# Sharing the opening's normalisations with ScalarE in a fused linear-attention and SwiGLU kernel, with the second tiles turned sooner and the first products issued part by part

## The chip, the cores and the metric

The kernel runs on one core of a Trainium2 chip. The metric is device microseconds (us) of one execution, as the median of several. One profiled execution gives the trace that is read here.

## The reference

One sequence of 2048 tokens with 1024 features is normalised, then goes through two branches whose outputs are multiplied and added to the input. The change touches only the first rows of the work: the normalisation `xn` and the first products of the gate and up projections.

```python
x  = A_x                                   # [1, 2048, 1024], f32
xn = (x - mean(x)) / sqrt(var(x) + 1e-5)   # layernorm over the 1024 features, no weights
# branch B, SwiGLU with F = 3584
h  = silu(xn @ w1) * (xn @ w3)
g  = silu(h @ w2)
# branch A, linear attention with 32 heads of 32
q, k, v = split(xn @ wqkv)
phi(t)  = concat(softmax(t @ w_phi), softmax(-(t @ w_phi)))     # per head
o = phi(q) (phi(k)^T v) / (phi(q) sum(phi(k)) + 1e-6)
return x + (o @ wo) * g
```

## The kernel before

**Products.** Every large matrix is cut into two by two blocks, and a block product is made from seven smaller ones instead of eight (a Strassen-Winograd scheme). The seven left operands of the tokens are called A11, A12, S2, S1, S3, S4 and A22, the right operands of the weights B11, B21, T2, T1, T3, B22 and T4; `ORDER` lists them with the PSUM bank (`a`, `b` or `c`) in which each is summed. To come near f32 accuracy each operand is kept as a high part (a cast to the matrix engine's f32 form) and a low part (what the cast left out, by a subtraction), and a product is three passes: high by high, low of the weights by high of the tokens, and high of the weights by low of the tokens. With four slices of the contraction that makes 12 matmuls of 128x512 for each product. `gate_up(step)` issues the 12 matmuls of product number `step`, and the function that it returns (kept in `reads`) issues the instructions that read the bank afterwards. "Product n" below is `gate_up(n)`. Each slice `f` of 128 columns takes seven products, one for each of A11 to A22. Bank `a` has one buffer, `b` and `c` have two each.

**The opening.** Tokens come in tiles of 128 rows. Tiles 0 to 3 (`xs[0]` to `xs[3]`) give A11 (their first 512 features, half 0) and A12 (half 1); tiles 4 to 7 give A21 and A22, from which S1, S2, S3 and S4 are summed. For each tile VectorE takes the mean and variance (`stats`), then ScalarE a square root and VectorE five small instructions give the reciprocal deviation (`rstd`, one for each group of four tiles), then `norm` subtracts the mean and scales, one instruction for each half. TensorE turns each half (`turn`: four 128x128 transposes into a PSUM bank), ScalarE casts the high part (`early_turn`), VectorE subtracts for the low part (`early_low`), and ScalarE also keeps an f32 copy (`early_raw`, or `raw_x` for tiles 4 to 7), which frees the bank. 36 transposes into `banka` that nobody reads run before that. The weights' operands are split the same way: `first_cast` casts on ScalarE, `first_low` subtracts on VectorE or on GpSimd; `b_operand` does both. `gpsimd_behind(src)` makes GpSimd wait until `src` is normalised.

**Order.** Throughout the gate and up products each engine runs its instructions in the order in which the program writes them, and so the place of a line sets what stands behind what: an instruction that waits holds back all that follow it on its engine. `OPENING` fixes which product is which. Products 0 to 4 multiply A11 or A12 by the first weight slices, product 7 is the first with S1, product 10 the first with S2, 12 and 13 the two with S3.

Of the kernel before, what the change touches and what calls it, by code (L numbers as in the profile page):

```python
# [10 lines left out]
AF = mybir.ActivationFunctionType  # L11
# [16 lines left out]
def tile_kernel(ctx: ExitStack, tc: tile.TileContext, x, wkT, wqT, wv, wphi, wo, w1, w3, w2, out):  # L28
    nc = tc.nc
# [184 lines left out]
    def norm(mv, sd, j, xt, halves=range(2)):  # L214

        for a in halves:
            nc.vector.tensor_scalar(xt[a], xt[a], mv[:, j, 0:1], sd[:, 1, j:j + 1], op0=OP.subtract, op1=OP.mult)
# [419 lines left out]
    def gate_up(step):  # L637
# [18 lines left out]
        if first:  # L656
# [3 lines left out]
                    kept_banks[f] = turned[0] % 3  # L660
            else:
                bank[b] = ps.tile([P, 512], F, name=f"bank{b}", bufs=BANKS[b])
        n = 0
        for k in range(4):
            for u, w in PASSES:
                nc.tensor.matmul(bank[b], bos[tb, f][bn][:, w, k], ao[an][:, u, k], start=first and n == 0,  # L666
                                 stop=LAST[b] == an and n == 11, skip_group_check=True)
# [77 lines left out]
    def first_b(f, n):  # L745
        b_operand(bos[0, f], ("B11", "B21")[n], raw_b[f][:, n])

    def first_cast(f, n):
        t = bos[0, f][("B11", "B21")[n]] = quad("bo")
        nc.scalar.copy(t[:, 0], raw_b[f][:, n].rearrange("p (k n) -> p k n", n=P))  # L750
# [20 lines left out]
    def early_raw(t, h):  # L771
        raw[t][early_at(t, h)[0]] = raw_x(pts.pop((t, h)))
# [3 lines left out]
    warm = ps.tile([P, 512], F, name="banka", bufs=BANKS["a"])  # L776
    for k in range(36):
        nc.tensor.transpose(warm[:, :P], xs[2 + min(k // 8, 1)][k // 4 % 2][:, k % 4 * P:k % 4 * P + P], ident)
# [12 lines left out]
    first_low(1, 0, nc.gpsimd)  # L791
    first_low(0, 1, nc.gpsimd)
    for t in range(4):
        early_low(t, 0)
    reads = [gate_up(0)]
    for t in range(4):
        early_raw(t, 0)
    for t in range(4):
        norm(mvs[0], sd, t, xs[t], (1,))
    gpsimd_behind(xs[3][1])  # L800
    first_low(1, 1, nc.gpsimd)
    stats(mvs[1], 0, xs[4])
    for t in range(4):
        early_turn(t, 1, **(in_c if t == 0 else {}))
# [25 lines left out]
    for t in range(4):  # L830
# [334 lines left out]
    bos = {}  # L1165
# [552 lines left out]
```

## Time and profile before

| | us |
|---|---|
| median of 3 runs | 2339.92 (2339.9 to 2340.1) |
| profiled execution, its own time | 2342.56 |
| span of its instructions | 2339.0 |
| busy TensorE | 2320.3 (99% of the span) |
| busy VectorE | 1825.2 (78%) |
| busy ScalarE | 889.0 (38%) |
| busy GpSimd | 258.6 (11%) |

In rows of the timeline the first number is the start in us from the span's first instruction, the second the length, then the engine, the line of the program, the operation, what it writes and reads, how many alike follow each other, and in brackets the idle time before it with what ended it. PE is TensorE, DVE VectorE, ACT ScalarE, POOL GpSimd.

### The profile page before, as it was taken

The page shows a single profiled execution, that of the slowest core. Times are in us where ns is not written, and L with a number is a line of the kernel's source. Part 1 is how long each engine was busy: PE and PEld are TensorE (multiplying, and loading weights), DVE is VectorE, ACT ScalarE, POOL GpSimd, SP SyncE. Part 2 cuts the span into 40 slices and gives each one's busy share as a digit, 9 for nine tenths or more (in the row PEclk, how much of TensorE's full clock was granted, in tenths as well). Part 3 has the DMA queues.
Part 4 walks back from the last instruction along what each step waited for, and adds up shares of the span by engine and source line. Part 5 has one row for each costly group of instructions (what it writes and reads, how often), then busy time and mean ns, then how long its engine had stood idle before and what let it go on. Part 6 is the DMA issues. An engine that isn't in the chain of part 4 may idle for free.

```text
span 2339.0 us, 33900 instructions
## 1 busy us (share of the span) xinstructions
PE 2320.3 (99%) x12754; PEld 1901.1 (81%) x12754; DVE 1825.2 (78%) x2854; ACT 889.0 (38%) x1561; POOL 258.6 (11%) x208
## 2 busy tenths in 40 slices
PE   8999999999999999999999999999999999999999
PEld 6778877788888888888888788888888888887787
DVE  8877788885688888875577777778688888887784
ACT  6445444443345554543222122334443333353000
POOL 1000000000000000000000000332022222211652
PEclk9999999999999999999999999999999999999999
DMA  3456789997788888866988978996644654379863
GB/s 129 158 197 218 246 302 370 346 322 225 240 278 307 299 305 298 285 230 217 379 293 280 336 230 319 331 363 233 205 153 135 207 180 135 133 250 278 234 186 104
DMA packets 302883, 580.93 MB, mean 248 GB/s; under 512 B 24696, under 2 KB 157184, under 8 KB 300032
## 3 DMA queue, kind: packets, MB, share of 16 engines
q1 hardware_dynamic: 296384, 555.70, 70.6%
q10 hardware_dynamic: 6336, 23.07, 2.5%
q8 instruction: 100, 1.64, 0.3%
q14 instruction: 63, 0.52, 0.1%
HBM read 375.78 MB, written 202.91 MB: 247 GB/s over the span
## 4 chain that ended last, share of the span: by engine, by line
PE 93%; DMA 3%; DVE 2%; ACT 1%; SPq 1%; issue 0%; DVEq 0%; ACTq 0%
PE bankb L666 26%; PE bankb L1441 13%; PE bankc L666 13%; PE bankb L951 7%; PE bankc L1441 6%; PE banka L666 6%; PE pm L1605 5%; PE bankb L1025 4%; PE bankc L951 3%; PE banka L1441 3%; PE bankc L1025 2%; PE banka L951 2%; DMA acc<-e_d 1%; PE banka L1025 1%; DMA wo_raw<-in_wo 1%; PE pkv L907 1%
## 5 line engine op out<-in xcount | busy, mean ns | idle before, releaser
L93 DVE TENSOR_TENSOR bo<-rw,bo 128x512 fp32r<-128x512 f32 x329 | 226.1, 688 | 144.9 <-ACT bo L92 144.5
L1441 PE MATMUL bankb<-bo,as 128*128 128x512 f32 x960 | 235.1, 389 | 0.0
L1441 PEld LDWEIGHTS bankb<-bo,as 128*128 128x128 f32 x960 | 180.2, 188 | 37.6
L92 ACT CAST bo<-rw 128x512 fp32r<-128x512 f32 x329 | 202.3, 618 | 20.8 <-DMA xo_d1A<-xoA 3.2
L994 POOL TENSOR_TENSOR eq<-q,mm 128x512 f32<-128x512 f32 x24 | 25.3, 1052 | 1514.3 <-DMA op4B<-wkv_d0B 1424.5
L666 PE MATMUL bankb<-op0S,bo 128*128 128x512 f32 x672 | 165.7, 396 | 4.5 <-ACT u L702 2.8
L666 PE MATMUL bankc<-op0S,bo 128*128 128x512 f32 x672 | 162.0, 390 | 0.0
L666 PE MATMUL bankb<-op1S,bo 128*128 128x512 f32 x672 | 161.2, 389 | 0.0
L666 PE MATMUL bankc<-op1S,bo 128*128 128x512 f32 x672 | 161.2, 389 | 0.0
L666 PE MATMUL bankb<-op0A,bo 128*128 128x512 f32 x672 | 159.2, 391 | 1.1 <-ACT op0A L765 0.8
L1441 PE MATMUL bankc<-bo,as 128*128 128x512 f32 x624 | 158.5, 389 | 0.2 <-DVE acc L1455 0.2
L666 PE MATMUL bankb<-op1A,bo 128*128 128x512 f32 x672 | 157.9, 390 | 0.0
L666 PEld LDWEIGHTS bankb<-op0S,bo 128*128 128x128 f32 x672 | 125.7, 189 | 37.0 <-issue 5.4
L1605 PE MATMUL pm<-wos,oT 128*128 128x512 f32 x651 | 153.7, 392 | 0.5 <-issue 0.3
L666 PEld LDWEIGHTS bankb<-op1A,bo 128*128 128x128 f32 x672 | 125.7, 188 | 28.2 <-DVE u L710 2.1
L666 PEld LDWEIGHTS bankc<-op0S,bo 128*128 128x128 f32 x672 | 125.6, 188 | 27.3 <-issue 1.2
L666 PEld LDWEIGHTS bankb<-op0A,bo 128*128 128x128 f32 x672 | 125.4, 188 | 27.5 <-ACT op0A L765 1.0
L666 PEld LDWEIGHTS bankc<-op1S,bo 128*128 128x128 f32 x672 | 126.1, 188 | 26.2
L666 PEld LDWEIGHTS bankb<-op1S,bo 128*128 128x128 f32 x672 | 126.1, 188 | 26.2
L1605 PEld LDWEIGHTS pm<-wos,oT 128*128 128x128 f32 x651 | 121.4, 188 | 28.2 <-issue 1.9
L1441 PEld LDWEIGHTS bankc<-bo,as 128*128 128x128 f32 x624 | 117.0, 188 | 24.9 <-DVE acc L1455 0.6
L717 ACT ACTIVATE h<-bankb 128x512 f32<-128x512 f32 x56 | 33.5, 598 | 237.6 <-PE bankb L666 237.6
(297 smaller groups left out, 4411.1 us busy)
## 6 DMA issues: line engine op xcount, KB each, us to landing
rw<-in_w SPq DMA_DIRECT2D x112, 512.0 KB, 5.9
hr<-h_d SPq DMA_DIRECT2D x56, 512.0 KB, 6.3
h_d<-h SPq DMA_DIRECT2D x108, 256.0 KB, 6.6
xoS<-xo_d0S SPq DMA_DIRECT2D x44, 512.0 KB, 5.3
xoS<-xo_d1S SPq DMA_DIRECT2D x44, 512.0 KB, 6.2
xoA<-xo_d0A SPq DMA_DIRECT2D x33, 512.0 KB, 5.7
xoA<-xo_d1A SPq DMA_DIRECT2D x33, 512.0 KB, 6.4
e_d<-eq ACTq DMA_DIRECT2D x32, 512.0 KB, 7.9
```

The source lines that it names most:

```text
L92: nc.scalar.copy(hi, src)
L93: (by or nc.vector).tensor_sub(lo, src, hi.bitcast(F))
L666: nc.tensor.matmul(bank[b], bos[tb, f][bn][:, w, k], ao[an][:, u, k], start=first and n == 0, stop=LAST[b] == an and n == 11, skip_group_c ...
L717: nc.scalar.activation(h1, bank["b"], AF.Silu)
L907: nc.tensor.matmul(pkv[sl, m], v[:, 4 * m + h], e[:, :, 4 * m + h], start=first and m == 0, stop=last, skip_group_check=True)
L951: nc.tensor.matmul(bank[b], xo[an][:, u, k], wb[bn][:, w, k], start=an in ("A11", "A12", "S1") and n == 0, stop=LAST[b] == an and n == 11, ...
L994: eng.tensor_sub(e[:, 0], p3, mm[:, 0, :].unsqueeze(2).to_broadcast([P, 16, DH]))
L1025: nc.tensor.matmul(bank[b], xo[an][:, u, k], wb[bn][:, w, k], start=an in ("A11", "A12", "S1") and n == 0, stop=LAST[b] == an and n == 11, ...
L1441: nc.tensor.matmul(bank[b], t[:, u, pos + k], bos[kb, bn, k][:, w], start=first and n == 0, stop=LAST[b] == an and n == 5, skip_group_chec ...
L1605: nc.tensor.matmul(p, oTs[t, h][:, a, k], wos[c, 4 * h + k][:, b], start=n == 0, stop=n == 3 * ND - 1)
```

## The change

Three things change in the opening, and nothing after product 15.

First, some halves are normalised on ScalarE in two instructions: `centre` adds the negated mean as soon as a tile's statistics are there (a third, tiny instruction negates the mean), and `scaled` multiplies by the reciprocal deviation later. Of tiles 0 to 3 this is half 0 of tiles 0 and 2 and half 1 of tiles 0 and 1; of the later tiles it is both halves of tile 4. The other halves stay on VectorE.

Second, lines move. The low part of the first weight operand is written behind the first two `norm`s instead of ahead of the small instructions of `rstd`; `stats` of tiles 5 to 7 and the rest of their `rstd` come ahead of the reads of products 0 to 3; the transposes of tiles 4 to 7 stand ahead of product 4 instead of behind it, and the read of product 4 stands behind the sums of S1. The order of GpSimd's two last low parts is swapped.

Third, the 12 matmuls of each of products 0 to 15 go pass by pass (four high by high, four with the weights' low part, four with the tokens' low part) instead of slice by slice.

```diff
-        n = 0
-        for k in range(4):
-            for u, w in PASSES:
-                nc.tensor.matmul(bank[b], bos[tb, f][bn][:, w, k], ao[an][:, u, k], start=first and n == 0,
-                                 stop=LAST[b] == an and n == 11, skip_group_check=True)
-                n += 1
+        passes = [(k, u, w) for u, w in PASSES for k in range(4)] if step < 16 else [(k, u, w) for k in range(4) for u, w in PASSES]
+        for n, (k, u, w) in enumerate(passes):
+            nc.tensor.matmul(bank[b], bos[tb, f][bn][:, w, k], ao[an][:, u, k], start=first and n == 0,
+                             stop=LAST[b] == an and n == 11, skip_group_check=True)
...
+    def centre(k, t, hs):
+
+        neg = consts[:, 2 + t:3 + t]
+        nc.scalar.activation(neg, mvs[k][:, t % 4, 0:1], AF.Copy, scale=-1.0)
+        for h in hs:
+            nc.scalar.activation(xs[t][h], xs[t][h], AF.Identity, bias=neg)
+
+    def scaled(sd, t, h):
+        nc.scalar.activation(xs[t][h], xs[t][h], AF.Copy, scale=sd[:, 1, t % 4:t % 4 + 1])
+
     for t in range(4):
         stats(mvs[0], t, xs[t])
-    def casts():
-        first_b(0, 0)
-        for f, n in ((1, 0), (0, 1), (1, 1)):
-            first_cast(f, n)
-
-    _, sd = rstd(mvs[0], sds[0], casts)
+        if t < 3:
+            centre(0, t, ((0, 1), (1,), (0,))[t])
+    r0, r1 = (rstd(mvs[k], sds[k]) for k in range(2))
+    next(r0)
+    first_cast(0, 0)
+    first_cast(1, 0)
+    sd = next(r0)
     for t in range(4):
-        norm(mvs[0], sd, t, xs[t], (0,))
+        if t % 2:
+            norm(mvs[0], sd, t, xs[t], (0,))
+        else:
+            scaled(sd, t, 0)
+    first_low(0, 0, nc.vector)
...
+    for t in range(2):
+        scaled(sd, t, 1)
...
     reads.append(gate_up(1))
     first_cast(2, 0)
+    first_cast(1, 1)
     first_low(2, 0, nc.gpsimd)
+    first_low(1, 1, nc.gpsimd)
     reads[0]()
-    for t in range(4):
+    centre(1, 4, (0, 1))
+    for t in range(2):
+        early_raw(t, 1)
+    for t in range(1, 4):
+        stats(mvs[1], t, xs[4 + t])
+    next(r1)
+    for t in range(2, 4):
         early_raw(t, 1)
     reads[1]()
     reads.append(gate_up(2))
     reads.append(gate_up(3))
-    for t in range(1, 4):
-        stats(mvs[1], t, xs[4 + t])
...
-    r1 = rstd(mvs[1], sds[1])
-    next(r1)
+    sd = next(r1)
+    for h in range(2):
+        scaled(sd, 4, h)
     reads[2]()
-    reads.append(gate_up(4))
-    sd = next(r1)
+    for t in range(1, 4):
+        norm(mvs[1], sd, t, xs[4 + t])
     first_b(3, 0)
+    first_cast(2, 1)
+    first_low(2, 1, nc.vector)
     reads[3]()
-    for t in range(4):
-        norm(mvs[1], sd, t, xs[4 + t])
-        if t == 1:
-            reads[4]()
+    next(gens[0, 0])
     for t in range(4, 8):
         if t == 7:
             first_sums("S1", (0, 1))
-            first_cast(2, 1)
-            next(gens[0, 0])
             first_split("S1", (0, 1))
         first_turn(t, 0, **(in_c if t % 2 else {}))
         first_turn(t, 1, **(in_c if t % 2 else {}))
+    reads.append(gate_up(4))
     reads.append(gate_up(5))
-    first_low(2, 1, nc.vector)
-    reads.append(gate_up(6))
     first_sums("S1", (2, 3))
     next(gens[0, 0])
     first_split("S1", (2, 3))
+    reads[4]()
+    reads.append(gate_up(6))
     next(gens[0, 1])
     first_b(3, 1)
     reads[5]()
```

TensorE's order around the transposes of tiles 4 to 7 (`late_x`), before. `banka_519` is product 4's bank, `bankb_486` product 3's, `bankb_611` product 5's.

```order
L666 MATMUL bankb_486<-op0A11_250,bo_459 128x512 x12
L666 MATMUL banka_519<-op0A12_251,bo_345 128x512 x12
L231 MATMUL pt_550<-ident_245,late_x_255 128x128 x4
L231 MATMUL pt_556<-ident_245,late_x_255 128x128 x4
L231 MATMUL pt_563<-ident_245,late_x_255 128x128 x4
...
L666 MATMUL bankb_611<-op0A11_250,bo_537 128x512 x12
```

The same place after the change, where `bankb_509` is product 3's bank and `banka_608` product 4's:

```order
L665 MATMUL bankb_509<-op0A11_250,bo_463 128x512 x12
L231 MATMUL pt_550<-ident_245,late_x_255 128x128 x4
L231 MATMUL pt_556<-ident_245,late_x_255 128x128 x4
L231 MATMUL pt_563<-ident_245,late_x_255 128x128 x4
...
L665 MATMUL banka_608<-op0A12_251,bo_465 128x512 x12
L665 MATMUL bankb_621<-op0A11_250,bo_542 128x512 x12
```

The 32 transposes moved ahead of product 4, which now stands between them and product 5.

VectorE's order around the second `rstd` and the reads of bank `a`, before. L696 is the read of a bank `a`: `banka_473` is product 2's, `banka_519` product 4's, `banka_625` product 6's.

```order
L696 TENSOR_TENSOR h0_462<-banka_473,h0_462 128x512
L206 RECIPROCAL consts_246<-consts_246 128x4
L208 TENSOR_TENSOR consts_246<-consts_246 128x4
...
L217 TENSOR_SCALAR late_x_255<-late_x_255,consts_246 128x512 x4
L696 TENSOR_TENSOR xt_259<-banka_519,xt_259 128x512
L217 TENSOR_SCALAR late_x_255<-late_x_255,consts_246 128x512 x4
...
L289 TENSOR_TENSOR rw_266<-rw_266,t2_514 128x512
L93 TENSOR_TENSOR bo_648<-room_b_254,bo_648 128x512
L696 TENSOR_TENSOR xt_257<-banka_625,xt_257 128x512
```

And after, where L694 is that read, `banka_496` is product 2's bank, `banka_608` product 4's and `banka_644` product 6's:

```order
L206 RECIPROCAL consts_246<-consts_246 128x4
L208 TENSOR_TENSOR consts_246<-consts_246 128x4
...
L694 TENSOR_TENSOR h0_469<-banka_496,h0_469 128x512
L217 TENSOR_SCALAR late_x_255<-late_x_255,consts_246 128x512 x6
...
L694 TENSOR_TENSOR xt_259<-banka_608,xt_259 128x512
L289 TENSOR_TENSOR rw_266<-rw_266,t2_525 128x512
L93 TENSOR_TENSOR bo_658<-room_b_254,bo_658 128x512
L694 TENSOR_TENSOR xt_257<-banka_644,xt_257 128x512
```

Two of the eight `norm`s left VectorE here, and the read of product 4 moved from between them to behind the sums of S1, where only two instructions stand between it and the read of product 6.

More of the change, by code (lines that the diff above doesn't have):

```diff
@@ L778, in tile_kernel @@
         nc.tensor.transpose(warm[:, :P], xs[2 + min(k // 8, 1)][k // 4 % 2][:, k % 4 * P:k % 4 * P + P], ident)
+    def centre(k, t, hs):
[5 more added lines that the diff above has]
+        nc.scalar.activation(xs[t][h], xs[t][h], AF.Copy, scale=sd[:, 1, t % 4:t % 4 + 1])
     for t in range(4):
         stats(mvs[0], t, xs[t])
-    def casts():
-        first_b(0, 0)
-        for f, n in ((1, 0), (0, 1), (1, 1)):
-            first_cast(f, n)
-    _, sd = rstd(mvs[0], sds[0], casts)
-    for t in range(4):
-        norm(mvs[0], sd, t, xs[t], (0,))
+        if t < 3:
[5 more added lines that the diff above has]
+    sd = next(r0)
+    for t in range(4):
+        if t % 2:
[3 more added lines that the diff above has]
+    first_low(0, 0, nc.vector)
+    for t in range(4):
         early_turn(t, 0, **(in_c if t == 3 else {}))
@@ L791, in tile_kernel @@
     first_low(1, 0, nc.gpsimd)
-    first_low(0, 1, nc.gpsimd)
+    for t in range(2):
+        scaled(sd, t, 1)
     for t in range(4):
@@ L795, in tile_kernel @@
     reads = [gate_up(0)]
+    for t in range(2, 4):
+        norm(mvs[0], sd, t, xs[t], (1,))
     for t in range(4):
         early_raw(t, 0)
-    for t in range(4):
-        norm(mvs[0], sd, t, xs[t], (1,))
+    first_cast(0, 1)
     gpsimd_behind(xs[3][1])
-    first_low(1, 1, nc.gpsimd)
+    first_low(0, 1, nc.gpsimd)
     stats(mvs[1], 0, xs[4])
@@ L808, in tile_kernel @@
     first_cast(2, 0)
+    first_cast(1, 1)
     first_low(2, 0, nc.gpsimd)
+    first_low(1, 1, nc.gpsimd)
     reads[0]()
-    for t in range(4):
+    centre(1, 4, (0, 1))
[4 more added lines that the diff above has]
+    next(r1)
+    for t in range(2, 4):
         early_raw(t, 1)
```

1 line of the change is left out of this document (removed).

## The prediction

> **What bounds the kernel now.** I read the page's first part, then who TensorE waited for, then the timelines of the first 90 us engine by engine.
>
> ```profile
> PE 2320.3 (99%) x12754; PEld 1901.1 (81%) x12754; DVE 1825.2 (78%) x2854; ACT 889.0 (38%) x1561; POOL 258.6 (11%) x208
> ```
>
> TensorE is busy for 2320.3 of 2339.0 us, so a change of the opening can only win or lose waits of TensorE there. Who it waited for, in total, times and longest:
>
> ```profile
> PE banka L778 <- DMA xt<-in_x: 7.2, 1, 7.2
> PE bankb L666 <- ACT u L702: 2.8, 1, 2.8
> PE bankb L666 <- ACT xt L702: 1.5, 1, 1.5
> PE bankb L666 <- ACT op0A L765: 0.8, 1, 0.8
> PE bankb L666 <- DVE op0A L769: 0.3, 1, 0.3
> ```
>
> TensorE's timeline has the places:
>
> ```profile
> 13.46 2.02 PE L231 MATMUL pt<-ident,xt 128*128 128x128 f32 x16
> 16.27 0.73 PE L666 MATMUL bankb<-op0A,bo 128*128 128x512 f32 x2 [0.78 <-ACT op0A L765]
> 17.31 2.56 PE L666 MATMUL bankb<-op0A,bo 128*128 128x512 f32 x10 [0.32 <-DVE op0A L769]
> 19.71 1.91 PE L231 MATMUL pt<-ident,xt 128*128 128x128 f32 x16
> 21.37 3.01 PE L666 MATMUL bankb<-op0A,bo 128*128 128x512 f32 x12
> ...
> 32.39 3.66 PE L231 MATMUL pt<-ident,late_x 128*128 128x128 f32 x32
> 35.80 3.01 PE L666 MATMUL bankb<-op0A,bo 128*128 128x512 f32 x12
> 38.65 3.21 PE L666 MATMUL banka<-op0A,bo 128*128 128x512 f32 x12
> ...
> 59.01 4.60 PE L666 MATMUL bankb<-op0S,bo 128*128 128x512 f32 x12 [2.82 <-ACT u L702]
> 65.09 3.02 PE L666 MATMUL bankb<-op0S,bo 128*128 128x512 f32 x12 [1.48 <-ACT xt L702]
> ...
> 81.55 2.88 PE L666 MATMUL bankc<-op0S,bo 128*128 128x512 f32 x12
> 84.27 2.88 PE L666 MATMUL bankb<-op0S,bo 128*128 128x512 f32 x12
> ```
>
> Undisturbed, a product takes 84.27 - 81.55 = 2.72. Between 16.27 (product 0) and 81.55 (product 19) lie 19 products and 48 transposes (21.37 - 19.71 = 1.66 and 35.80 - 32.39 = 3.41): 51.7 + 5.1 = 56.8 of work in 65.3 us. About 8.5 us are lost, most at products 12 and 13 (59.01 and 65.09). From 65.09 on TensorE runs dense, so the kernel's time moves by what product 13's start moves.
>
> Product 12 also ran slowly, 4.60 for 12 matmuls. The row of the windows names span, busy time of PE, PEld, DVE, ACT and POOL, then the granted clock:
>
> ```profile
> 59.60:63.00 3.40, 3.40 (x10) 2.64 (x9) 3.30 (x6) 0.62 (x2) 0.00 (x0) 0.52 0.00 0
> ```
>
> After a wait of 2.82 the clock was about half for 3.4 us; after the 1.48 ahead of 65.09 it stayed full. The slow stretch cost nothing here, because product 13 waited anyway.
>
> What does product 13 wait for? VectorE's and ScalarE's timelines:
>
> ```profile
> 12.06 0.16 DVE L208 TENSOR_TENSOR consts<-consts 128x4 f32<-128x4 f32 x1
> ...
> 14.78 2.48 DVE L769 TENSOR_TENSOR op0A<-pt,op0A 128x512 fp32r<-128x512 f32 x4
> ...
> 20.96 2.48 DVE L769 TENSOR_TENSOR op0A<-pt,op0A 128x512 fp32r<-128x512 f32 x4 [0.36 <-ACT op0A L765]
> 23.36 1.28 DVE L194 BATCH_NORM_STATS2 st<-late_x 128x6 f32<-128x512 f32 x2
> ...
> 27.59 0.65 DVE L696 TENSOR_TENSOR h<-banka,h 128x512 f32<-128x512 f32 x1
> 28.15 0.17 DVE L206 RECIPROCAL consts<-consts 128x4 f32<-128x4 f32 x1
> 28.35 1.22 DVE L208 TENSOR_TENSOR consts<-consts 128x4 f32<-128x4 f32 x1
> ...
> 30.70 1.92 DVE L217 TENSOR_SCALAR late_x<-late_x,consts 128x512 f32<-128x512 f32 x4
> ...
> 35.02 1.28 DVE L343 TENSOR_TENSOR room_b<-room_a,xf 128x512 f32<-128x512 f32 x2
> ...
> 43.15 0.68 DVE L696 TENSOR_TENSOR xt<-banka,xt 128x512 f32<-128x512 f32 x1
> ...
> 59.80 2.49 DVE L352 TENSOR_TENSOR xf<-xf,room_a 128x512 f32<-128x512 f32 x4
> ```
>
> ```profile
> 2.04 0.20 ACT L775 ACTIVATE consts<-consts 128x1 f32<-128x1 f32 x1
> 10.41 0.30 ACT L202 ACTIVATE consts<-consts 128x4 f32<-128x4 f32 x1 [8.17 <-DVE consts L196]
> ...
> 14.16 2.05 ACT L765 CAST op0A<-pt 128x512 fp32r<-128x512 f32 x4 [1.38 <-PE pt L231]
> ...
> 54.25 0.63 ACT L865 ACTIVATE xt<-xt 128x512 f32<-128x512 f32 x1 [0.34 <-DVE xt L696]
> ...
> 62.38 2.18 ACT L92 CAST op0S<-xf 128x512 fp32r<-128x512 f32 x4 [2.90 <-DVE xf L352]
> 64.47 0.57 ACT L702 COPY xt<-bankb 128x512 f32<-128x512 f32 x1
> ```
>
> Product 13 sums into the bank of product 11, which ScalarE reads at 64.47; in ScalarE's queue that read stands behind the casts of S4 (62.38), and these wait for VectorE's sums (59.80). VectorE has had almost no idle time since 11 us. So the chain is VectorE's list, 65.09 - 43.15 = 21.94 long from its read of product 6's bank (L696 at 43.15) to product 13. After that read both orders hold the same work, so the question is when the changed kernel reaches it.
>
> **Step by step.** *Product 0.* The tokens' low parts (done at 14.78 + 2.48 = 17.26) are wanted only by the last four matmuls, 8 x 0.227 = 1.8 after 16.27. The wait of 0.32 and the broken start go: product 0 ends at 16.27 + 2.72 = 18.99 instead of 19.71, **0.7 earlier**. The start itself stays: the four casts (14.16 + 2.05 = 16.21) follow the transposes at 13.46, and the halves that ScalarE scales are due only by then. ScalarE's `centre` instructions fill its idle 8.17 us ahead of 10.41, so they cost nothing.
>
> *Products 1 to 3* then run from 18.99 + 1.66 = 20.65 to 28.81, without a wait: their casts and GpSimd's low parts move up with the turning.
>
> *The transposes of tiles 4 to 7* now stand here, and TensorE reaches them at 28.8 instead of 32.39. They need ScalarE's `scaled` of tile 4, and that needs the second `rstd`. VectorE subtracts the second low parts 0.7 earlier, to 22.7; `stats` of three tiles take 27.59 - 23.36 = 4.2, to 26.9; square root (0.30) and reciprocal bring L208 to about 27.5. Alone, the last four small instructions take 0.2 each, as L208 did at 12.06, and the deviation would be there at 28.3. But at 28.35 the same instruction took 1.22. GpSimd's rows say why:
>
> ```profile
> 22.99 1.30 POOL L754 TENSOR_TENSOR bo<-room_b,bo 128x512 fp32r<-128x512 f32 x1 [2.28 <-ACT bo L750]
> 24.25 1.31 POOL L129 TENSOR_TENSOR rw<-rw 128x512 f32<-128x512 f32 x1
> ...
> 28.26 1.29 POOL L131 TENSOR_TENSOR t<-rw 128x512 f32<-128x512 f32 x1
> ```
>
> L208 began 0.09 after a GpSimd subtraction or sum and ended with it (29.57 against 29.55). [...]
>
> In the changed kernel GpSimd has six such instructions in one run instead of five (the swapped low part joins them). They start when ScalarE has cast `first_cast(2, 0)`, at about 22.2, and five took 29.55 - 22.99 = 6.6, so six take 7.9, to 30.0: the fifth from 27.3, the sixth from 28.7. L208 at 27.5 falls into the fifth, and one of L209 and L211, which have two operands too, into the sixth. The deviation is there at about 30.3 instead of 28.3, `scaled` (0.63 like L865, or 0.1 more for an operand by pointer, as 0.30 against 0.20 in the two small activations) ends at 31.1, and TensorE begins at 31.2, after **a wait of 2.4**.
>
> The transposes need 3.41, but the fifth half needs a bank that ScalarE frees. ScalarE still has the second `scaled`, two casts and a read, to 33.2, then copies at about 0.5 each; the fifth transposes go at 33.85, the eighth end at 35.75. That is before's 35.80, with product 4 (2.72) still to do: TensorE is 2.7 behind here.
>
> *Product 6* comes after 4 and 5, at 41.2 at best instead of 38.65, and needs bank `a`, which VectorE frees by its read of product 4. That read moved behind S1: from 30.3 VectorE does one read (0.6), six `norm`s (6 x 0.46 = 2.8), three subtractions (1.8), then ten instructions of S1 at 0.6 and some waits of about 0.5, and reads product 4 between 41.0 and 42.1. Product 6 starts near 41.9 and ends at 44.7. VectorE's read of it, two instructions after that of product 4, waits until about 44.85, where it came to its turn at 43.15 before: **1.7 later**. What the `norm`s gave VectorE is idle time here.
>
> *From there on* the list is the same 21.94 to product 13: 66.8 instead of 65.09, and the rest runs dense. The waits ahead of products 12 and 13 are for reads of their banks, so going pass by pass gives nothing there. The first transfers in SP's queue that wait for an engine are these, behind the part that changes:
>
> ```profile
> 62.96 7.80 SPq L260 DMA_DIRECT2D rw<-in_w  x4
> ```
>
> They bring the weights of product 18 and later, and move with the list. Sum: **+1.7 us**. On the profiled execution (2342.56, span 2339.0, so 3.6 around it) that is 2344.3; on the median of 2339.92 it is **2341.6**. A measurement of this kernel can tell about 0.2% (4.7 us) from no change, so this counts as none.
>
> Bounds: no row shows an activation with a full operand by pointer; at 0.63, without the 0.1 that I add, two on the chain take 0.2 off, and at twice 0.1 they put 0.2 on. If GpSimd's run ends 0.4 earlier or later than 30.0, so does the hold. From +1.0 to +2.3.
>
> **The rivals.** *The half clock at the new wait.* TensorE's wait of 2.4 is near the 2.82 that halved the clock and above the 1.48 that did not. If it does, 3.4 us of transposes and product 4 run at half speed and lose 1.7; this time product 6 is on the path, and most of it arrives: +3.3, 2343.2. [...]
>
> *Slower by more than can be measured.* [...] If product 12 runs at full speed (2.72 instead of 4.60), it ends 1.9 sooner and the gap ahead of 13 is 1.48 + 1.9 = 3.4, more than the 2.82 that halved the clock; then products 13 and 14 lose 1.7, on the path. With the 1.7 at the transposes that is 1.7 + 1.7 + 1.7 = +5.1, 2345.0. It decides from the point where both gaps halve the clock and that ahead of product 12 does not.
>
> *No hold by GpSimd.* The deviation comes at 28.3, the transposes start at 29.1, product 6 ends at 42.65, and VectorE reads it at 42.85: -0.3, 2339.6. For it: one instruction more or less on GpSimd's side shifts the meeting. Against it: GpSimd's run leaves no gap of over 0.1 between its instructions.
>
> *The relief arrives.* Six halves less on VectorE are 6 x 0.46 = 2.8; if the read of product 6 finds its product done, product 13 comes up to 2.8 sooner: 2337.1. Against it stands the order: the reads of 4 and 6 have two instructions between them and a product takes 2.72.
>
> **How the numbers follow.** +1.7 at full clock 0.45; half clock at the new wait 0.28; no hold 0.14; slower by over 0.2% 0.07; relief 0.06, of which 0.02 beyond 0.2%. Predicted: 2341.6. The range leaves out the relief and the worst clock: 2339.3 to 2344.3. Within 0.2%: 0.45 + 0.28 + 0.14 + 0.04 = 0.91.
>
> **What would show it.** Right: product 0 without a gap; a wait of TensorE of 2 to 3 us ahead of the transposes of `late_x`, put down to ScalarE; L208 and another small instruction of about 1 us beside GpSimd; an idle time of VectorE of 1.5 to 2 us ahead of the read of product 6's bank; product 13 near 66.8. The half clock would show as a granted clock near 0.5 behind 31 us. Wrong: transposes that start before 30, or product 13 ahead of 65.

## The result and the profile after

| | us |
|---|---|
| the changed kernel, median of 22 runs | 2343.65 (2340.63 to 2346.18) |
| the kernel before on the same chips, median of 22 runs | 2340.57 (2339.52 to 2343.24) |
| ratio | 1.0012, 95% interval 1.0006 to 1.0017 |
| span of the profiled execution, before and after | 2339.0 and 2342.1 |

The change costs about 3 us, 0.13%: inside the range, within the 0.2% that was set as no change, and slower in sign as forecast. The interval leaves out 1, so 22 runs of each do tell so small a loss from none. Who TensorE waited for in the changed kernel, in total, times and longest:

```profile
PE bankb L665 <- ACT xt L700: 3.0, 1, 3.0
PE bankb L665 <- ACT u L700: 2.3, 1, 2.3
PE pt L231 <- ACT late_x L785: 2.1, 1, 2.1
PE bankb L665 <- ACT op0A L763: 0.8, 1, 0.8
```

The waits inside product 0 are gone, a new one of 2.1 stands ahead of the transposes of `late_x`, and that ahead of product 13 has grown from 1.5 to 3.0. TensorE's timeline:

```profile
16.23 3.04 PE L665 MATMUL bankb<-op0A,bo 128*128 128x512 f32 x12 [0.83 <-ACT op0A L763]
19.10 1.91 PE L231 MATMUL pt<-ident,xt 128*128 128x128 f32 x16
...
31.27 5.56 PE L231 MATMUL pt<-ident,late_x 128*128 128x128 f32 x32 [2.06 <-ACT late_x L785]
36.59 3.00 PE L665 MATMUL banka<-op0A,bo 128*128 128x512 f32 x12
...
42.15 2.96 PE L665 MATMUL banka<-op0A,bo 128*128 128x512 f32 x12
...
61.02 3.06 PE L665 MATMUL bankb<-op0S,bo 128*128 128x512 f32 x12 [2.31 <-ACT u L700]
67.10 5.49 PE L665 MATMUL bankb<-op0S,bo 128*128 128x512 f32 x12 [3.02 <-ACT xt L700]
72.38 6.05 PE L665 MATMUL bankc<-op0S,bo 128*128 128x512 f32 x24
78.27 5.60 PE L665 MATMUL bankb<-op0A,bo 128*128 128x512 f32 x24
```

VectorE's rows, and those of GpSimd beside them:

```profile
27.67 1.18 DVE L208 TENSOR_TENSOR consts<-consts 128x4 f32<-128x4 f32 x1
28.89 0.16 DVE L209 SCALAR_TENSOR_TENSOR consts<-consts 128x4 f32<-128x4 f32 x1
29.08 1.12 DVE L210 TENSOR_SCALAR consts<-consts 128x4 f32<-128x4 f32 x1
30.24 0.16 DVE L211 TENSOR_TENSOR consts<-consts 128x4 f32<-128x4 f32 x1
...
41.35 0.69 DVE L694 TENSOR_TENSOR xt<-banka,xt 128x512 f32<-128x512 f32 x1
45.15 0.69 DVE L694 TENSOR_TENSOR xt<-banka,xt 128x512 f32<-128x512 f32 x1 [1.91 <-PE banka L665]
```

```profile
27.55 1.28 POOL L129 TENSOR_TENSOR rw<-rw 128x512 f32<-128x512 f32 x1
28.91 1.27 POOL L131 TENSOR_TENSOR t<-rw 128x512 f32<-128x512 f32 x1
```

Two of the four small instructions end with a GpSimd instruction (28.85 against 28.83, 30.20 against 30.18). The deviation is there at 30.4, TensorE has waited since 29.2, and VectorE later stands idle for 1.91 ahead of its read of product 6 (45.15).

That is the forecast's chain, and it puts product 13 at 67.10, 2.0 behind the kernel before. What product 16 loses beyond that is the clock: the row of the windows gives span, busy times of PE, PEld, DVE, ACT and POOL, then the granted clock.

```profile
32.50:36.00 3.50, 3.50 (x19) 3.50 (x18) 3.50 (x7) 3.36 (x8) 0.00 (x0) 0.54 0.01 2
66.60:73.50 6.90, 6.40 (x16) 5.01 (x17) 6.80 (x12) 3.80 (x8) 0.00 (x0) 0.52 0.41 148
```

Products 13 to 15 take 78.27 - 67.10 = 11.17 instead of 73.39 - 65.09 = 8.30, so product 16 starts 4.9 late. Of these 4.9 the end of the run shows 3.1: 0.7 goes where the kernel before itself waited, for a transfer, and the rest in two more places of under 0.8 each near 2192 and 2248 us. The kernel before at the first of these places:

```profile
1138.93 3.01 PE L951 MATMUL bankb<-op2B,xoA 128*128 128x512 f32 x12 [0.53 <-DMA xoA<-xo_d0A]
```

Runs of one kernel lie up to 6.7 us apart here. More time at half clock does not explain it: of the changed kernel's 22 runs the 7 with a mean granted clock of 0.999 took 2344.3 on average, the 15 with 0.998 took 2343.0. So each experiment has a median of 8 to 11 runs beside its one profile.

### The profile page after: what moved, and what is told of

It is laid out like the page before. It is cut to its first block, busy times and chain, and to the rows that moved or that the text cites. A ratio compares the mean times of both kernels' runs of the same rounds, so it can differ in the third digit from the quotient of the medians.

```text
span 2342.1 us, 33907 instructions
## 1 busy us (share of the span) xinstructions
PE 2321.8 (99%) x12754; PEld 1903.8 (81%) x12754; DVE 1824.4 (78%) x2848; ACT 897.5 (38%) x1577; POOL 258.5 (11%) x208
## 3 DMA queue, kind: packets, MB, share of 16 engines
q8 instruction: 100, 1.64, 0.3%
## 4 chain that ended last, share of the span: by engine, by line
PE 96%; DVE 1%; DMA 1%; ACT 1%; issue 0%; SPq 0%; DVEq 0%; ACTq 0%
PE bankb L665 26%; PE bankc L665 13%; PE bankb L1462 13%; PE pm L1626 7%; PE bankb L972 7%; PE bankc L1462 6%; PE banka L665 6%; PE bankb L1046 4%; PE bankc L972 4%; PE banka L1462 3%; PE bankc L1046 2%; PE banka L972 2%; PE banka L1046 1%; DMA wo_raw<-in_wo 1%; PE po L1607 1%; PE pkv L928 1%
```

## The experiments

Times are medians in us beside the kernel before on the same chip; P13 and P16 are the starts of products 13 and 16 in the profile, to be read against product 0, whose start differs by up to 1.3 us between profiles. The ratio is taken from the runs and can differ from the quotient of the two medians by up to 0.0005 (1.1 us), so smaller differences of medians say nothing.

| kernel | time | before | ratio, 95% interval | span | P0 | P13 | P16 |
|---|---|---|---|---|---|---|---|
| before | | | | 2339.0 | 16.27 | 65.09 | 73.39 |
| changed | 2343.65 | 2340.57 | 1.0012, 1.0006 to 1.0017 | 2342.1 | 16.23 | 67.10 | 78.27 |
| e1, passes alone | 2342.60 | 2340.72 | 1.0004, 0.9995 to 1.0013 | 2338.8 | 16.30 | 64.57 | 72.88 |
| e2, no hold | 2340.41 | 2340.72 | 0.9999, 0.9990 to 1.0007 | 2338.6 | 16.73 | 65.54 | 73.81 |
| e3, turned later | 2341.64 | 2340.72 | 1.0000, 0.9992 to 1.0009 | 2341.1 | 16.57 | 64.68 | 75.69 |
| e4, gaps filled | 2346.65 | 2340.72 | 1.0025, 1.0016 to 1.0035 | 2345.4 | 16.48 | 67.10 | 75.39 |
| e5, filled with 128 | 2343.21 | 2340.44 | 1.0009, 1.0001 to 1.0018 | 2341.2 | 17.06 | 67.66 | 75.96 |
| e6, no sharing | 2345.94 | 2340.44 | 1.0019, 1.0010 to 1.0028 | 2344.5 | 16.66 | 68.12 | 79.24 |
| e7, reads first | 2338.82 | 2340.44 | 0.9993, 0.9983 to 1.0002 | 2336.8 | 16.44 | 58.89 | 69.52 |
| e8, all | 2337.47 | 2340.44 | 0.9986, 0.9977 to 0.9995 | 2334.6 | 15.80 | 57.13 | 69.38 |
| e9, changed and 58 | 2347.27 | 2341.09 | 1.0028, 1.0018 to 1.0038 | 2345.1 | 16.50 | 67.37 | 77.07 |
| e10, before and 58 | 2344.05 | 2341.09 | 1.0014, 1.0005 to 1.0023 | 2345.9 | 17.14 | 65.97 | 77.00 |
| e11, all and 20 | 2337.19 | 2341.09 | 0.9983, 0.9974 to 0.9992 | 2335.4 | 16.07 | 57.64 | 68.39 |

**e1: the pass-by-pass order alone, on the kernel before.**

```diff
+        passes = [(k, u, w) for u, w in PASSES for k in range(4)] if step < 16 else [(k, u, w) for k in range(4) for u, w in PASSES]
+        for n, (k, u, w) in enumerate(passes):
```

> The kernel before with only the pass-by-pass order of products 0 to 15. Theory (waits): product 0 loses its break of 0.3 and ends about 0.6 us earlier (the turning behind it at 19.1 instead of 19.7), but product 13 waits for the read of its bank, which hangs on VectorE's list, so it starts 0 to 0.6 earlier (64.5 to 65.1) and the time is 0 to 0.6 us lower than before. Rival (order itself costs): the passes change TensorE's pace or make product 13 later, and part of the loss of 3 us shows here.

Product 0 ran without a break and its transposes came at 19.21 instead of 19.71. Product 13 got all of the 0.5, and the time cannot be told from the kernel before. TensorE's rows of products 12 and 13:

```profile
58.49 4.61 PE L665 MATMUL bankb<-op0S,bo 128*128 128x512 f32 x12 [3.33 <-ACT u L700]
64.57 3.03 PE L665 MATMUL bankb<-op0S,bo 128*128 128x512 f32 x12 [1.47 <-ACT xt L700]
```

**e2: the changed kernel without the hold.** The sums of slice f=1 go from GpSimd to VectorE, just ahead of their use.

```diff
+    late_sums = []
...
-        b_sums(rw[0], rw[2], rw[3], t2, nc.gpsimd)
+        late_sums.append((rw[0], rw[2], rw[3], t2))
+        if f == 0:
+            b_sums(*late_sums.pop(), nc.gpsimd)
...
     reads.append(gate_up(6))
+    b_sums(*late_sums.pop())
     next(gens[0, 1])
```

> The changed kernel with the two sums of the second weight slice taken from GpSimd to VectorE, written just ahead of their use, so that GpSimd is done at about 27.6, when the second deviation is computed. Theory (GpSimd holds VectorE's small instructions): L208 and L210 take 0.2 instead of 1.2 and 1.1, the transposes of tiles 4 to 7 start at about 29.5 instead of 31.3 and TensorE waits 0.5 or less instead of 2.1; the two sums (1.2) fit into VectorE's idle 1.9 ahead of the read of product 6. Product 13 at about 65.2 instead of 67.1, the time 1.5 to 3.5 us below the changed kernel's (the waits of 1.9 and what half clock they brought). Rival (ScalarE's share is late by itself): the small instructions get short, but the transposes still start at 31 or later and product 13 stays at 67.

VectorE's rows, then TensorE's:

```profile
28.16 0.16 DVE L208 TENSOR_TENSOR consts<-consts 128x4 f32<-128x4 f32 x1
...
28.55 0.17 DVE L210 TENSOR_SCALAR consts<-consts 128x4 f32<-128x4 f32 x1
...
43.60 0.69 DVE L694 TENSOR_TENSOR xt<-banka,xt 128x512 f32<-128x512 f32 x1 [0.46 <-PE banka L665]
```

```profile
30.04 2.14 PE L231 MATMUL pt<-ident,late_x 128*128 128x128 f32 x16 [0.30 <-ACT late_x L785]
...
65.54 2.99 PE L665 MATMUL bankb<-op0S,bo 128*128 128x512 f32 x12 [1.72 <-ACT xt L700]
```

With no GpSimd instruction beside them both take 0.16 to 0.17, the wait shrinks from 2.06 to 0.30, VectorE's idle time from 1.91 to 0.46, although VectorE now does two sums more, and the 3 us are gone. With the hold the loss goes, so it is the cause of at least the 2 us at product 13. Products 13 to 15 also ran at full clock here (73.81 - 65.54 = 8.27, in the kernel before 8.30), but that is not shown to come from the missing hold: in this profile product 12 ran partly at half clock (4.36 instead of 3.06, granted clock 0.64 from 60 to 63 us), and this shortened the gap ahead of product 13 to 1.72.

**e3: the hold stays, but product 4 stands ahead of the transposes again**, so that TensorE has work while the deviation is late.

```diff
+    reads[2]()
+    reads.append(gate_up(4))
     sd = next(r1)
     for h in range(2):
         scaled(sd, 4, h)
-    reads[2]()
...
     reads[3]()
+    reads[4]()
...
-    reads.append(gate_up(4))
...
-    reads[4]()
```

> The changed kernel with product 2's read and product 4 put ahead of the second deviation and the transposes again, and product 4's read ahead of the sums of S1. Theory: product 4 (2.7) covers the wait for tile 4, TensorE waits less than 0.3 ahead of the transposes (at about 31.8), VectorE does not wait for product 6 (idle under 0.3 instead of 1.9), and VectorE's list reaches that read near 43.3. Product 13 at about 65.3, as before the change, the time 1.5 to 3.5 us below the changed kernel's: the hold of 2 us still eats what the shared normalisations gave. Rival (ScalarE's extra instructions are the loss): the order makes no difference, product 13 at 67.

TensorE's rows:

```profile
32.13 1.91 PE L231 MATMUL pt<-ident,late_x 128*128 128x128 f32 x16
...
58.60 3.02 PE L665 MATMUL bankb<-op0S,bo 128*128 128x512 f32 x12 [3.08 <-ACT u L700]
64.68 5.49 PE L665 MATMUL bankb<-op0S,bo 128*128 128x512 f32 x12 [3.07 <-ACT xt L700]
```

TensorE's rows show no wait ahead of the transposes, and product 13 comes 2.4 sooner than in the changed kernel, though L208 and L210 were held as long (1.09 and 1.15). So the hold costs product 13 nothing where TensorE has other work. Behind a wait of 3.07 products 13 to 15 run largely at half clock (75.69 - 64.68 = 11.01 instead of 8.30, granted clock 0.62 from 63 to 72 us), as in the changed kernel, and product 16 is 2.3 later than in the kernel before. The median is 0.9 over the kernel before and the ratio 1.0000, where 1.5 to 3.5 under the changed kernel was expected: that came out.

**e4: the half clock taken away** by transposes of the constant that nobody reads: 16 ahead of those of tiles 4 to 7, 18 ahead of product 12, 24 ahead of product 13.

```diff
...
+        if step in (12, 13):
+            spin = ps.tile([P, 512], F, name="spin", **tr_bank())
+            for k in range(18 if step == 12 else 24):
+                nc.tensor.transpose(spin[:, :P], ident, ident)
```

> The changed kernel with transposes of the identity that nobody reads in TensorE's three gaps: 16 ahead of the transposes of tiles 4 to 7, 18 ahead of product 12, 24 ahead of product 13. They change no wait. Theory: the waits cost 1.5 to 2.0 us (product 13 at 66.5 to 67.1) and the rest of the 3 us, with the spread of 5.5 us between runs, is the half clock that gaps bring; with the gaps filled the granted clock stays full, the median is 1 to 2 us below the changed kernel's (about 1.5 above before) and the runs lie within 2 us. Rival (no part of it is the clock): time and spread as the changed kernel's.

TensorE's rows:

```profile
67.10 3.01 PE L671 MATMUL bankb<-op0S,bo 128*128 128x512 f32 x12 [0.44 <-ACT xt L706]
...
2137.95 1.68 PE L1613 MATMUL po<-acc,kvs 64*32 64x64 f32 x125
2142.45 0.42 PE L1613 MATMUL po<-acc,kvs 64*32 64x64 f32 x3 [2.83 <-issue]
```

A miss. The opening did as expected: full clock, product 13 at 67.10 and product 16 2.9 us sooner than in the changed kernel. But the median is 5.9 us over the kernel before, where the changed kernel is 3.1 over it, and the runs lie 4.2 us apart, not within 2. Most of it is lost at 2142 us, where TensorE stops for 2.83 us in a run of 128 small matmuls, with no releaser (TensorE's rows above), and the clock halves behind it (rows of the windows; the last three columns are the clock, the share of the DMA engines and GB/s).

```profile
2138.00:2142.00 4.00, 1.63 (x126) 1.32 (x126) 2.42 (x3) 0.59 (x1) 0.00 (x0) 1.00 1.00 387
2142.00:2145.40 3.40, 2.95 (x9) 2.29 (x9) 1.87 (x3) 0.59 (x1) 0.00 (x0) 0.53 1.03 420
```

In the changed kernel the same 128 matmuls run through:

```profile
2138.57 1.71 PE L1607 MATMUL po<-acc,kvs 64*32 64x64 f32 x128
```

**What happened at 2142 us.** The page's row of the instruction queue (packets, MB, share of the DMA engines' time) in the kernel before and in e4:

```profile
q8 instruction: 100, 1.64, 0.3%
```

```profile
q8 instruction: 101, 1.65, 0.3%
```

TensorE's 12,754 matmuls and as many weight loads make 25,508 instructions. If the 100 packets are their code, 1.64 MB are some 64 bytes for each, and a packet, 16,384 bytes in the trace, holds some 256: an estimate of mine from these numbers. The 128 small matmuls with their loads are 256 instructions in 1.7 us: by the estimate a whole packet, at a time when the DMA engines are full (share 1.00 from 2138 to 2142 us in e4). The 116 instructions of e4 would have moved the packet's end into this run. That is a theory; e5, e9 and e10 test it.

**e5: 128 such transposes, 256 instructions, so that by the estimate every later packet begins at the instruction at which it began in the changed kernel.**

```diff
...
+    for k in range(38):
+        nc.tensor.transpose(warm[:, :P], ident, ident)
     for k in range(36):
         nc.tensor.transpose(warm[:, :P], xs[2 + min(k // 8, 1)][k // 4 % 2][:, k % 4 * P:k % 4 * P + P], ident)
+    for k in range(23):
+        nc.tensor.transpose(warm[:, :P], ident, ident)
...
+        spins = {12: 21, 13: 27}.get(step, 0)
```

> Like the kernel of e4, but with 128 transposes of the constant that nobody reads instead of 58: 38 ahead of the 36 warming ones and 23 behind them (TensorE stands idle in both places), 19 ahead of the transposes of tiles 4 to 7, 21 ahead of product 12 and 27 ahead of product 13. What is open: e4 held the clock in the opening and had product 16 2.9 us earlier than the changed kernel, yet came out 3 us later, with a stop of TensorE of 2.8 us at about 2140 us that the profile puts down to nothing but issue. Theory: TensorE's code comes in packets (100 of them for 1.64 MB and 25,508 matmuls and weight loads, so some 256 instructions each), e4's 116 further instructions moved the places where a packet is needed, and one of them fell where all 16 DMA engines were full. Then 256 further instructions move every place by just one packet: no stop near 2140 us, product 13 at about 67.1 us and product 16 at about 75.4 us at full clock, one packet more on the queue, and a time of 2339.5 to 2342 us. Rival: a clock that is kept up in the opening is taken away later, whatever the places of the packets are; then a half-clock stretch and a loss of 4 to 6 us come late in the run again, and the time is 2345 to 2348 us.

No stop near 2140 us; e4's late loss is gone. Its time, though, is 1.2 us over the top of what was expected. Product 16 is 3.1 us sooner after product 0 than in the changed kernel, and of that 0.3 us remain in the median (each against the kernel before on its chip) and 0.9 in the span, or 1.7 if one counts back that product 0 started 0.8 later in e5. In the profile most of what goes is lost at one place, in another stop without a releaser, at 2250 us, which the changed kernel's profile does not have. TensorE's waits in e5 name it:

```profile
PE pm L1637 <- issue: 1.2, 1, 1.2
```

Up to there e5 was still 1.9 us ahead of the changed kernel, behind it 0.7. So what the half clock in the opening is worth at the end stays open: 0.3 us by the medians, 1.7 by the profiles, and up to 1.2 more than that if the stop is chance.

**e9 and e10: 58 such transposes where TensorE is idle anyway, ahead of product 0**, on the changed kernel and on the kernel before; nothing is filled later.

```diff
+    for k in range(38):
+        nc.tensor.transpose(warm[:, :P], ident, ident)
     for k in range(36):
...
+    for k in range(20):
+        nc.tensor.transpose(warm[:, :P], ident, ident)
```

> The changed kernel with 58 transposes of the constant that nobody reads, as many as in e4, but all of them where TensorE stands idle ahead of product 0: 38 ahead of the 36 warming ones, 20 behind them. Nothing is filled later, so the waits ahead of the transposes of tiles 4 to 7 and of products 12 and 13 stay. Theory (e4's late loss comes from where TensorE's code packets end, 116 instructions further on): a stop of TensorE of 2 to 3 us with no releaser at about 2140 us, as in e4, and a time 2 to 4 us over the changed kernel, 2345.5 to 2347.5 us. Rival (e4's loss came from holding the clock up, or from chance): no such stop, and the changed kernel's time, 2342.5 to 2344.5 us.

> The kernel before with the same 58 transposes of the constant ahead of product 0 and nothing else changed. Theory (packet places): the opening as before (product 13 at about 65.1 us), the stop at about 2140 us appears here too, 2 to 4 us over the kernel before: 2342.5 to 2344.5 us. Rival: within 0.5 us of the kernel before.

TensorE's rows in e9, then in e10:

```profile
2137.65 1.71 PE L1611 MATMUL po<-acc,kvs 64*32 64x64 f32 x128
2142.16 2.33 PE L1630 MATMUL pm<-wos,oT 128*128 128x512 f32 x5 [2.79 <-DMA g<-g_d]
```

```profile
2139.00 1.70 PE L1590 MATMUL po<-acc,kvs 64*32 64x64 f32 x127
2142.80 0.21 PE L1590 MATMUL po<-acc,kvs 64*32 64x64 f32 x1 [2.11 <-issue]
```

The stop comes back in both, within three matmuls of the same place. Against the kernel before on its chip e9 is 6.2 us over, the changed kernel 3.1: as the theory had it, with up to 0.3 from product 0, which started that much later. In e9 the profile names a transfer as releaser; the waiting matmul reads `wos` and `oT`, not `g`, and `oT` was done at 2140.8, so I take it for the same stop.

e10 is 3.0 over, but its opening was not that of the kernel before, though this was expected: product 0 started 0.9 later, and its rows of products 12 and 13 show a wait of 2.84 that left the clock full and one of 3.06 that halved it, where in the kernel before 2.82 halved it and 1.48 did not.

```profile
59.89 3.02 PE L666 MATMUL bankb<-op0S,bo 128*128 128x512 f32 x12 [2.84 <-ACT u L702]
65.97 5.49 PE L666 MATMUL bankb<-op0S,bo 128*128 128x512 f32 x12 [3.06 <-ACT xt L702]
```

Product 16 is 3.6 late there, so the 3.0 are not shown to be the stop's alone. The 7 of e10's 11 runs with a mean clock of 0.999, which all 24 runs of the kernel before beside it have, are 2.1 over it on average.

The trace also has the packets of the instruction queue one by one. In e4 one begins at 2140.18, when TensorE has stood since 2139.63, and lands at 2141.15; TensorE goes on at 2142.45. In e9 one lands at 2140.60 and TensorE goes on at 2142.16, in e10 at 2141.36 and 2142.80. Smaller stops that the profile puts down to issue are in the profiles of the kernel before, e1 to e3 and e5 to e8 (0.3 to 1.2 us, between 2243 and 2254 us) and of e11 (0.8 at 2144 us); the changed kernel's has none. That of the kernel before ends at 2247.98, behind a packet that lands at 2246.45. At all twelve TensorE stands 173 to 193 matmuls and weight loads behind a multiple of 256, and goes on 1.2 to 1.6 us after a packet lands. So the place in the code decides where, by this count. Why TensorE still waits that long is not shown; that it is because the DMA engines are full there (share 1.00 in e4, 1.02 in e9 and 0.99 in e10) is an inference.

**e6: the changed kernel with the normalisations of tiles 0 to 4 back on VectorE.**

```diff
-        if t < 3:
-            centre(0, t, ((0, 1), (1,), (0,))[t])
...
-        if t % 2:
-            norm(mvs[0], sd, t, xs[t], (0,))
-        else:
-            scaled(sd, t, 0)
+        norm(mvs[0], sd, t, xs[t], (0,))
...
```

> The changed kernel with all its normalisations of tiles 0 to 4 back on VectorE (the order of steps and passes stays). Theory (GpSimd's hold makes the new wait, the sharing is worth little): the two held instructions stay at about 1.1 us each, the wait ahead of the transposes of tiles 4 to 7 is 2.0 to 2.7 us, product 6 starts at 42.2 to 42.7, product 13 at 67.1 to 67.6, and the time is that of the changed kernel, 0 to +0.5 us. Rival (ScalarE's share delays the second deviation or the reads): the wait shrinks below 1.5 us and product 13 comes before 66.3 us.

TensorE's row:

```profile
32.13 5.35 PE L231 MATMUL pt<-ident,late_x 128*128 128x128 f32 x32 [2.52 <-DVE late_x L217]
```

The wait stays (2.52 in TensorE's row), so the sharing does not cause it. Product 13 is 0.6 later after product 0 than in the changed kernel: a little more than expected, and the sharing is worth that. The median is 5.5 us over the kernel before (4.4 by the ratio), 2.4 more than the changed kernel, where 0 to 0.5 were expected. In the profile 1.4 of it come behind 2190 us, 0.9 of these at a stop of the kind seen in e5, near 2253 us; the rest is open.

**e7: ScalarE's reads first.** The kernel before with the new order of passes, and with ScalarE's silus and its casts for S4 and A22 called after later products, so that the reads of products 10 and 11 stand ahead of them.

```diff
...
-    at(9, first_silus)
-    at(11, lambda: first_late("S4"))
-    at(12, lambda: first_late("A22"))
+    at(12, lambda: first_late("S4"))
+    at(13, lambda: first_late("A22"))
+    at(13, first_silus)
```

> The kernel before, with the changed kernel's order of passes, and with ScalarE's silus and its casts for S4 and A22 moved behind its reads of products 10 and 11 (called after products 12 and 13). Theory: the wait of about 3 us ahead of product 12 is ScalarE standing in other work when the bank is full, so products 12 and 13 start 3 and 6 us earlier (about 55.8 and 58.5 us), but VectorE's work is then late and takes most of it back: product 14 at about 63.8 with a wait of 2.5 us ahead of it, product 16 about 2 us and product 30 about 1.2 us ahead of the kernel before; time 0.5 to 1.5 us under it. Rival: the wait only changes its place, product 30 within 0.3 us of before, time the same.

TensorE's row:

```profile
63.95 5.74 PE L665 MATMUL bankc<-op0S,bo 128*128 128x512 f32 x24 [2.18 <-ACT op0S L92]
```

As in the theory, the two waits of 2.8 and 1.5 give way to one of 0.8 ahead of product 12, one of 2.2 ahead of product 14 (TensorE's row) and one of 1.0 behind it. Product 13 is 6.2 sooner, product 16 3.9, product 30 2.6 (1.2 were expected), the median 1.6, just short of what can be told from no change.

**e8: together.** The changed kernel with the order of e3, the reads of e7, and GpSimd's sums of slice f=0 issued sooner.

```diff
+    sums_of(0)
...
-    for f in range(2):
-        rw, t2 = first_rws.pop(0), work.tile([P, 512], F, name="t2", tag="w")
-        b_sums(rw[0], rw[2], rw[3], t2, nc.gpsimd)
-        gens[0, f] = b_others(rw, bos[0, f], t2)
+    sums_of(1)
+    reads[2]()
+    reads.append(gate_up(4))
...
```

> The changed kernel with what the other runs point to: product 2's read and product 4 ahead of the second deviation (as in e3), GpSimd's first two sums issued two steps sooner so that they are out of the way of one of the two held instructions, and ScalarE's silus and casts behind its reads of products 10 and 11 (as in e7). Theory: no new wait ahead of the transposes of tiles 4 to 7, products 12 and 13 at about 54.7 and 57.4 us, a wait of 2.5 us ahead of product 14, product 30 at about 110 us, some 2.4 us ahead of the kernel before; time 2338 to 2339.5 us, or 1.7 us more if a half-clock stretch follows the wait ahead of product 14. Rival: work behind product 30 does not pass the gain on (the loss of the changed kernel shrank by 1.8 us there as well), and the time is within 0.5 us of the kernel before.

VectorE's rows, then TensorE's:

```profile
27.34 0.16 DVE L208 TENSOR_TENSOR consts<-consts 128x4 f32<-128x4 f32 x1
...
27.73 1.15 DVE L210 TENSOR_SCALAR consts<-consts 128x4 f32<-128x4 f32 x1
```

```profile
54.24 5.78 PE L665 MATMUL bankb<-op0S,bo 128*128 128x512 f32 x24 [0.22 <-ACT u L700]
...
62.26 7.28 PE L665 MATMUL bankc<-op0S,bo 128*128 128x512 f32 x24 [2.25 <-ACT op0S L92]
```

One of the two holds is left and is covered; products 12 and 13 follow product 11 with a wait of 0.2. It beats both kernels: 0.14% under the kernel before, with 1 outside the interval, and 0.5 us under the lowest time expected, although the clock fell once more behind the wait ahead of product 14 (0.79 from 62 to 70 us where it was 1.00 from 50 to 62, and 24 matmuls in 7.28 where e7 took 5.74).

**e11: e8 with 20 transposes of the constant in that wait.**

```diff
+        if step == 14:
+            spin = ps.tile([P, 512], F, name="spin", **tr_bank())
+            for k in range(20):
+                nc.tensor.transpose(spin[:, :P], ident, ident)
```

> The kernel of e8 with 20 transposes of the constant in its one wait of 2.3 us, ahead of product 14 (40 TensorE instructions, a sixth of a code packet). Theory: no half-clock stretch behind that wait, product 16 at about 67.8 instead of 69.4 us; by what holding the clock through the opening brought in the fifth run, 0.4 to 1 us of the 1.6 are left at the end: 2336 to 2337.2 us, unless a packet's place falls badly. Rival: the places of the packets decide, and the time is over that of e8.

TensorE's rows:

```profile
62.81 5.73 PE L669 MATMUL bankc<-op0S,bo 128*128 128x512 f32 x24
...
70.06 5.28 PE L669 MATMUL bankb<-op0A,bo 128*128 128x512 f32 x22 [1.05 <-DVE op0A L93]
...
2144.54 0.38 PE L1613 MATMUL po<-acc,kvs 64*32 64x128 f32 x2 [0.83 <-issue]
```

The clock stays up, as TensorE's rows show, but TensorE then waits 1.05 for VectorE's next low part, which eats what was won: product 18 starts 59.1 after product 0, in e8 59.0. And e11, which has 40 TensorE instructions more than e8, has a stop of 0.83 at 2144 us that e8 does not have there; so the place in the code costs something here too, as the rival had it, though the time is not over that of e8. At 0.9983 (0.9974 to 0.9992) it cannot be told from e8.

## Why the prediction was right, and where not

- *Product 0*: 0.6 earlier at its transposes, 0.7 forecast. Right; e1 shows it alone.
- *The wait at the transposes*: 2.06 instead of 2.4, since TensorE came there at 29.2, not 28.8; the deviation at 30.4 (30.3 forecast), the transposes at 31.27 (31.2). Right, and shown by e2 to come from GpSimd.
- *Which instructions are held*: L208 as said. The second was to be one of L209 and L211, with two operands; it was L210, which reads one. That step named the wrong instruction and had the right time by the same meeting: L208 and L210 each start in a GpSimd instruction and end with it (28.85 against 28.83, 30.20 against 30.18). That two operands are what gets an instruction held, no run shows: in the kernel before L208 alone of the four met a GpSimd instruction and was held (1.22), here L210 was too (1.12, against 0.17 in e2).
- *Product 6 and VectorE's read of it*: 42.15 and 45.15, forecast 41.9 and 44.85; idle time 1.91, forecast 1.5 to 2. Right.
- *Product 13*: 67.10, forecast 66.8. Right, 0.3 more; from VectorE's read of product 6's bank to product 13 it took 67.10 - 45.15 = 21.95, forecast 21.94, and 21.94 in e2.
- *"The rest runs dense"*: wrong in its words. Products 13 to 15 ran at half clock in the profile and product 16 was 4.9 late, more than the +1.7 of the sum. That is the mechanism of the rival of slower by more than can be measured (product 12 at full speed, hence a longer gap, hence the half clock), over two stretches instead of one. That rival's price of +5.1 was not reached, as the loss at product 16 did not all come to the end. Whether an execution meets this stretch is luck as far as the record goes: in e10's profile the kernel before met it too, and in e9's profile the changed kernel's product 13 took 4.42 and its products 14 and 15 ran at full clock.
- *The half clock at the new wait*: it came (0.54 from 32.5 to 36.0 us), and was priced at +1.6 over the likeliest case. From product 0 to product 6 the changed kernel takes 25.92, e5 without the half clock 42.64 - 17.06 = 25.58, as the row of e5 below shows: only 0.3, because at full clock TensorE waits instead: in e5 0.46 among the transposes for ScalarE's copies and 0.34 ahead of product 6 for VectorE.

```profile
42.64 3.03 PE L672 MATMUL banka<-op0A,bo 128*128 128x512 f32 x12 [0.34 <-DVE xt L701]
```

- *The size*: +3.1 measured, +1.7 forecast. The hold's part was 2.0 at product 13, close to the forecast. The rest, about 1, would be the clock behind product 13, which the likeliest case had at nothing; that split is not shown. e5, at full clock, is still 2.8 over the kernel before, with 0.8 of a later product 0 in it, and the changed kernel's own runs are not faster at a higher mean clock. So the step on the hold was right, and that the total still lies inside the range owes something to luck.

## What to carry to other kernels

Work that is moved ahead must have its inputs ahead too: here the transposes came sooner, and what they needed hung on four tiny VectorE instructions beside GpSimd, so either keep GpSimd quiet there (e2) or keep other work for TensorE in between (e3). An engine that frees a bank for a waiting one should not stand in other work: putting two reads ahead of casts and silus brought product 13 forward by 6.2 us (e7), and of all the kernels only the two that have it together with e3's order (e8, e11) are told from the kernel before as faster. A difference of 0.1% between two kernels can come from where instructions fall in the code (e9: 58 transposes, all ahead of product 0, 3.1 us over the changed kernel, with a stop of 2.79), so look for a stop without a releaser before explaining it otherwise.

## What the runs showed of the hardware

- Of the small instructions of four elements, one with a single input (L210) was held by GpSimd as the one with two was: 1.12 against 0.17 alone. The reciprocal (L206), also with one input, was not: 0.17 inside a GpSimd instruction in e8 (27.13, beside 26.16 to 27.47).
- 116 TensorE instructions, most of them in idle time, brought a stop of 2.1 to 2.8 us 2.1 ms later (e4, e9, e10) and, in e9, 3 us of loss over the changed kernel; with 256 there was none at that place (e5), though one of 1.2 us came at 2250 us. All twelve such stops lie 173 to 193 TensorE instructions behind a multiple of 256 and end 1.2 to 1.6 us after a packet of the instruction queue lands; that a packet holds 256 is an estimate.
- Waits of TensorE of 2.06 and 2.25 were followed by a lower clock (0.50 from 32.3 to 35.7 us in the changed kernel, 0.79 from 62 to 70 us in e8), one of 2.31 ahead of product 12 was not in the changed kernel (product 12 in 3.06) and was in e2 (2.30, product 12 in 4.36); 2.82 was in the kernel before (0.50 from 59.5 to 62.9 us), and 2.84 was not in e10 (product 12 in 3.02), the same kernel with transposes ahead of product 0. The length of the wait alone does not decide; what does is not shown. The slow stretches took 3.4 us in the kernel before and 3.4 and 6.7 us (0.50 from 66.5 to 73.2 us) in the changed kernel.
- Transposes of a constant kept the clock full through waits of 2 to 3 us (granted clock 1.00 from 60 to 64 us in e4 and 58 to 77 in e5; in e11 the 24 matmuls behind them took 5.73, in e8 without them 7.28).
